# Attention inside a fused kernel: sums read out of PSUM at another place, softmax sums over groups of three tiles, and a new spread of small work over two engines

## The chip, the core and the metric

One core of one Trainium2 chip runs the whole program. The metric is device time in microseconds, the median of three runs of the compiled program. Where a profile is quoted, its times are microseconds from the first instruction of one profiled execution, and durations in groups are mean nanoseconds of one instruction. PE is TensorE's matmul side, PEld its weight loads, DVE is VectorE, ACT is ScalarE, POOL is GpSimd and SP issues transfers.

## The reference, cut to what matters

Attention comes first, then a mixture of experts, then a second feed-forward part. Only attention is touched. It has 2 x 8 heads, 1152 keys, 576 pooled queries and a head size of 64:

```python
q_pool = q.reshape(B, H, S // 2, 2, D).mean(axis=3)
scores = scale * np.matmul(q_pool, k.transpose(0, 1, 3, 2))
scores = scores - np.max(scores, axis=-1, keepdims=True)
attn = np.exp(scores)
attn = attn / (np.sum(attn, axis=-1, keepdims=True) + 1e-09)
return np.matmul(attn, v)
```

## The kernel before, in words

Heads are worked on in eight pairs, `p` 0 to 7. A pair has nine steps `t`, one for each tile of 128 keys; the loop over `g` at the end of the attention part runs through all of them and writes the program in the order in which the engines' queues will hold it. Each engine works its queue strictly in that order, so a waiting instruction holds up all that stands behind it.

In step `t` of pair `p` stand, in this order on PE: the scores of tile `t` (`scores`, eight products), two "chunks", the products of the previous tile's exponentials with `v` (`pv`, into the one PSUM buffer `pv` that a pair has), sometimes the sums of exponentials (`psums`), and the remaining chunks. ACT turns scores into exponentials `pt`.

A chunk (`max_chunk`) is a product of queries and keys of the *next* pair, from which the row maxima are found. There are 27 chunks to a pair, in units of three: nine units, four blocks of queries of head 0, four of head 1, and one of both heads' remainders (two products to a chunk). Of a unit's three chunks DVE reduces one (line 103), ACT takes the positive part of one (`wd<-mx`), and DVE joins the third with it (line 239, called `ISA` in the program's order and `CUSTOM_DVE_ANT_0` in the trace; a short read of the accumulator follows). The chunks lie in three PSUM buffers `mx`. When all are through, `max_cols` makes the maxima and their remainders on DVE (`mfin`, `Mt`), and in step 8 `max_rows` transposes them on PE (line 269) and copies them with ACT into `qb`, where the next pair's scores need them.

Work between the chunks is put there by a table: `at_step(p, t, ...)` gives step `t` of pair `p` a task, and each chunk slot takes one task ahead of its chunk; what is left over is done at the step's end. Tasks are the preparation of the next pairs' queries and keys (`qhi`, `qlo`, `khi`, `klo`, `kdiff`, `qcopy`), `max_cols`, the reciprocal of the sums and the output of the pair before (`sum_rec`, `x_out`), and the decoding of weights for a later stage (`decode`, three parts to a block, on DVE with one ACT instruction `dm<-wraw`). `qlo` writes the lower half of the query tile `qs` on DVE (line 97, `qs<-tq,qs`); a head's first chunk needs it. In the last pair there are no chunks, and three decode parts stand in each step.

The sums of exponentials need a product with a matrix of ones for each tile (`psums`, line 323: 16 PE records for one pass). To save passes, DVE adds tiles ahead (`st`): tiles 0 and 1, 2 and 3, 4 and 5. So a pair has six passes, three over `st` and three over tiles 6, 7 and 8. When the last tile is through, in step 0 of the next pair, `post_evac` moves products and sums out of `pv`: two ACT reads (`wd<-pv`, `sm<-pv`) and a DVE addition (`sm<-pv,sm`). The next pair's first `pv` product, in its step 1, has to wait for all three. Before the change this stands at the very end of step 0:

```python
for f in tasks:
    f()
if t == 0 and p > 0:
    post_evac(p - 1)
```

The functions and the loop:

Of the kernel before, what the change touches and what calls it, by code (L numbers as in the profile page):

```python
# [9 lines left out]
F32 = mybir.dt.float32  # L10
# [4 lines left out]
AF = mybir.ActivationFunctionType  # L15
ALU = mybir.AluOpType
# [68 lines left out]
def kernel(ctx, tc, cst, qt, kt, v, wgo, w1, w2, wio, out):  # L85
# [4 lines left out]
    def act(out, in_, func=AF.Copy, **kw):  # L90
        A.activation(out=out, in_=in_, func=func, **kw)  # L91

    def tt(eng, out, a, b, op):
        eng.tensor_tensor(out=out, in0=a, in1=b, op=op)  # L94
# [80 lines left out]
        SP.dma_start(out=vt[p], in_=v[p])  # L175

    DEC_M = 32
    DEC_T, DEC_A = [0, 1, 3, 5, 7, 8], 23
    tqt = {}

    def qsum(p, h):
# [13 lines left out]
    def qcopy(p, h):  # L195
        QB[p, h] = ap.tile([P, SQ], F32R, name="qb", bufs=NBL)
        act(QB[p, h][:64], QS[p, h][:64].bitcast(F32))

    def khi(p, h, c):
        if c == 0:  # L200
            At[p, h] = ap.tile([P, S], F32R, name="at", bufs=NB)
        cs_ = slice(c * SQ, (c + 1) * SQ)
        act(At[p, h][:, cs_], kd[p, h][:, cs_])

    def klo(p, h, c):
        cs_ = slice(c * SQ, (c + 1) * SQ)
        tt(G if 2 * p + h < 3 else V, Bt[(2 * p + h) % NBL][:64, cs_], kd[p, h][:64, cs_], At[p, h][:64, cs_].bitcast(F32), ALU.subtract)
# [33 lines left out]
    def ahead(units):  # L241
        n = len(units)
        seq_ = [(units[0], 0), (units[0], 1)]
        for i in range(n):
            if i + 1 < n:
                seq_ += [(units[i + 1], 1)]
            seq_ += [(units[i], 2)]
            if i + 1 < n:
                seq_ += [(units[i + 1], 0)]
        return [(*u, c) for u, c in seq_]  # L250

    chunks = ahead([(h, j) for h in range(2) for j in range(4)])
    mchunks = ahead([(0, 4)])
    chunks0 = ahead([(h, j) for h in range(2) for j in range(4)] + [(0, 4)])

    mfin = {}

# [47 lines left out]
            mm(pvt[p][64 * h:64 * h + 64, f, :HQ], lhsT=vt[p][:, t, h, :], rhs=Pt[p, t][:, h, f * HQ:(f + 1) * HQ], start=t == 0, stop=t == KT - 1, skip_group_check=True)  # L305


    twos = (1, 3, 5)
    St = {}

    def add_two(p, t):
        St[p] = ap.tile([P, 2, SQ], F32, name="st", bufs=1)
        tt(V, St[p], Pt[p, t - 1], Pt[p, t], ALU.add)

    def psums(p, t):


        for src in ([St[p]] if t - 1 in twos else []) + ([] if t in twos or t + 1 in twos else [Pt[p, t]]):
            for f in range(2):
                for h in range(2):  # L320
                    for a in range(2):
                        q_, t0 = 64 * h + 32 * a, 256 * a + 160 * f
                        mm(pvt[p][q_:q_ + 32, f, HQ:HQ + 160], lhsT=e2[:, h], rhs=src[:, h, t0:t0 + 160], start=False, stop=src is Pt.get((p, KT - 1)), skip_group_check=True)
# [108 lines left out]
    def load_raw(i, pool):  # L432
        f, c = divmod(i, 2)
        wraw[i] = pool.tile([P, 512, 2], I32, name="wraw", bufs=2)
        (SP if pool is ap else A).dma_start(out=wraw[i].rearrange("p a b -> p (a b)"), in_=wio[f, :, 512 * c:512 * (c + 1)].bitcast(I32))

    def decode(i, part, pool):
        f, c = divmod(i, 2)
        lo, hi = wraw[i][:, :, 0], wraw[i][:, :, 1]
        dst = wd[f][:, 512 * c:512 * (c + 1)]  # L440
        if part == 0:
            m = dmt[i] = pool.tile([P, 512], F32, name="dm", bufs=2)
            s = dst_[i] = pool.tile([P, 512], I32, name="ds", bufs=1)
            act(m, hi.bitcast(F32), AF.Abs)
            ts(V, s, hi, -0x80000000, ALU.bitwise_and)
        m, s = dmt[i], dst_[i]
        mi = m.bitcast(I32)
        if part == 1:
            ts(V, m, m, F_LO, ALU.max, F_HI, ALU.min)
            stt(s, lo, 29, s, ALU.logical_shift_right, ALU.bitwise_or)  # L450
        if part == 2:
            ts(V, mi, mi, 3, ALU.logical_shift_left, 0x40000000, ALU.bitwise_xor)
            stt(dst.bitcast(I32), mi, 0x7FFFFFFF, s, ALU.bitwise_and, ALU.bitwise_or)


    T_S, T_T, T_R, T_X = [2, 4, 5, 6]
    sched = {}

    def at_step(p, t, *fns):
        sched.setdefault(9 * p + t, []).extend(fns)  # L460
# [3 lines left out]
    at_step(-1, 4, lambda: (qcopy(0, 0), klo(0, 1, 1)))  # L464
    at_step(-1, 5, lambda: qcopy(0, 1))
    for p in range(NPAIR):
        for h, (a, b) in enumerate((((p - 2, 4), (p - 1, 0)), ((p - 1, 0), (p - 1, 3)))):
            lp, lt = (a[0], 2) if h == 0 else (p - 2, 6)
            if p == 0:
                continue  # L470
            if (p, h) == (1, 0):
                at_step(-1, 1, lambda: load_k(1, 0))
                at_step(-1, 6, lambda: (qsum(1, 0), khi(1, 0, 0), kdiff(1, 0)))
                at_step(-1, 7, lambda: qhi(1, 0))
                at_step(-1, 8, lambda: max_cols(0), lambda: qlo(1, 0))
                at_step(0, 0, lambda: khi(1, 0, 1), lambda: (klo(1, 0, 0), qcopy(1, 0)))
                at_step(0, 1, lambda: klo(1, 0, 1))
                continue
            at_step(lp, lt, lambda p=p, h=h: load_k(p, h))
            at_step(*((p - 2, 4 * h) if p > 1 else (lp, lt)), lambda p=p, h=h: load_q(p, h))  # L480
            at_step(a[0], a[1], lambda p=p, h=h: (qsum(p, h), khi(p, h, 0)))
            at_step(a[0], a[1] + 1, lambda p=p, h=h: (qhi(p, h), khi(p, h, 1), kdiff(p, h)))
            at_step(a[0], a[1] + 2, lambda p=p, h=h: qlo(p, h))
            at_step(b[0], b[1], lambda p=p, h=h: (klo(p, h, 0), qcopy(p, h)))
            at_step(b[0], b[1] + 1, lambda p=p, h=h: klo(p, h, 1))
        at_step(p - 1, 6, lambda p=p: load_v(p))
        if p:
            at_step(p - 1, 8, lambda p=p: max_cols(p))
        if p < NPAIR - 1:
            at_step(p + 1, T_R, lambda p=p: sum_rec(p))  # L490
            at_step(p + 1, T_X, lambda p=p: x_out(p, 0))
            at_step(p + 1, T_X + 1, lambda p=p: x_out(p, 1))
            at_step(p + 2, 1, lambda p=p: x_put(p))
# [68 lines left out]
    for g in range(-9, 9 * NPAIR):  # L562
        p, t = divmod(g, 9)
        if t == 0:
            todo = list(chunks if p >= 0 else chunks0) if p + 1 < NPAIR else []
            mtodo = list(mchunks) if 0 <= p < NPAIR - 1 else []
        tasks = list(sched.get(g, ()))
        if p >= 0 and t - 1 in twos:
            tasks += [lambda: None] * (2 - len(tasks))
            tasks.insert(2, lambda p=p, t=t: add_two(p, t - 1))  # L570
        if p == NPAIR - 1:
            tasks.append(lambda: [(raw_ahead(ap, DEC_A), decode_step(ap, DEC_A)) for _ in range(3)])
        elif p >= 0 and t in DEC_T:
            tasks.append(lambda: (raw_ahead(ap, DEC_A), decode_step(ap, DEC_A)))

        slot = [0]

        def mxc(todo=todo):
            if tasks:
                tasks.pop(0)()  # L580
            if todo:
                max_chunk(p + 1, *todo.pop(0))
            slot[0] += 1

        prev = divmod(g - 1, 9)
        seq = "0mmrpsmMt" if p < NPAIR - 1 else "0mmrpsmmt"
        if g < 0:
            seq = "mmmm"
        assert not (t == 8 and (todo or mtodo)), (p, len(todo), len(mtodo))
        if t < 3:  # L590
            seq = seq.replace("M", "m")
        for ch in seq:
            if ch == "0":
                if p >= 0:
                    scores(p, t)
            elif ch == "m":
                mxc()
            elif ch == "M":
                if mtodo:
                    mxc(mtodo)  # L600
                else:
                    mxc()
            elif ch == "s":
                if p > 0 and t == T_S:
                    sum_log(p - 1)
            elif ch == "t":
                if p > 0 and t == T_T:
                    sum_tr(p - 1)
            elif ch == "e":
                mxc([])  # L610
            elif ch == "r":
                if t == 8 and 0 <= p < NPAIR - 1:
                    max_rows(p + 1)
            elif ch in "pfg" and prev[0] >= 0:
                if ch in "pf":
                    pv(*prev, 0)
                if ch in "pg":
                    pv(*prev, 1)
                    psums(*prev)
        for f in tasks:  # L620
            f()
        if t == 0 and p > 0:
            post_evac(p - 1)
        if p > 0 and t in (T_X - 1, T_X):
            x_tr(p - 1, t - T_X + 1)
        if g == -1:
# [770 lines left out]
```

## Time and profile before

| | |
|---|---|
| median of 3 runs | 691.95 us (691.91 to 692.37) |
| the profiled execution | 689.39 us, its span 687.6 us |
| pairs 1 to 6, from one pair's transposes of maxima to the next | 205.06 us, 34.18 us each |
| busy in those: PE, DVE, ACT | 197.93, 154.73, 147.36 us |
| mean granted clock of the span | 0.988 of full speed, 1.00 in the pairs 1 to 6 |

Attention takes the first 298 us of the span. PE is the fullest engine in it, so it is read by PE's timeline: where PE stands still, and which instruction's end lets it go on. A start in the timeline less the start before it is what an instruction costs its engine; the duration in the row is longer where the next one overlaps. The times between pairs are the starts of line 269 in step 8: 20.96, 52.16, 86.20, 120.67, 154.66, 189.22, 223.49 and 257.22.

### The profile page before, as it was taken

To read this page: it belongs to the slowest core of one execution; us is meant where nothing else is said; L and a number is where in the kernel's file an instruction comes from. 1 tells how busy PE (TensorE), PEld (TensorE's weight loads), DVE (VectorE), ACT (ScalarE), POOL (GpSimd) and SP (SyncE) were. 2 spreads that over 40 slices of the span, in tenths; PEclk is the share of its full clock that TensorE was granted. 3 is DMA by queue.
4 is the path that set the end of the run, shared out by engine and by line. 5 is a ranking of instruction groups with operands and counts; after the bars stand their busy time and mean duration, and the time that the engine had idled before them with its cause. 6 is when DMAs were issued, how large, how long until landed. Compare 5 with 4: busy or idle time off the path is not lost. (4 is left out here: it accounts for less than half of the span.)

```text
span 687.6 us, 11646 instructions
## 1 busy us (share of the span) xinstructions
PE 636.9 (93%) x4335; PEld 499.2 (73%) x4335; DVE 498.4 (72%) x1035; ACT 401.6 (58%) x825; POOL 155.9 (23%) x155
## 2 busy tenths in 40 slices
PE   4899999999999999849989999987999999999997
PEld 3776767676767675528877977757787999999995
DVE  5686869686969686965753967514999977897775
ACT  7878585858585857514344546524665554555543
POOL 7500110101010000023222523302222332233222
PEclk9899999999999999989999999999999999999999
DMA  7853444444442313439489877660000020001001
GB/s 268 279 136 130 107 152 99 148 107 148 101 142 73 113 27 120 140 119 352 143 281 398 294 277 291 241 242 20 0 1 2 1 92 1 1 0 47 1 1 47
DMA packets 26643, 88.35 MB, mean 128 GB/s; under 512 B 2886, under 2 KB 7631, under 8 KB 22482
## 3 DMA queue, kind: packets, MB, share of 16 engines
q1 hardware_dynamic: 21264, 73.23, 30.4%
q0 software_dynamic: 3568, 8.79, 5.6%
q10 hardware_dynamic: 1746, 5.51, 2.4%
q8 instruction: 36, 0.59, 0.3%
q14 instruction: 29, 0.24, 0.1%
HBM read 79.65 MB, written 8.39 MB: 128 GB/s over the span
## 5 line engine op out<-in xcount | busy, mean ns | idle before, releaser
L91 ACT ACTIVATE pt<-sc 128x320 f32<-128x320 f32 (+1 forms) x216 | 96.1, 488 | 30.1 <-PE sc L290 25.8
L100 POOL TENSOR_SCALAR u<-u 128x384 f32<-128x384 f32 x48 | 60.3, 1257 | 151.9 <-ACT u L91 117.2
L305 PE MATMUL pv<-pt,vt 128*64 128x288 f32 x576 | 86.1, 420 | 7.3 <-issue 5.5
L866 PE MATMUL zps<-yh,wh 128*128 128x384 f32 x188 | 64.1, 341 | 1.7 <-DVE n L97 1.7
L868 PE MATMUL zps<-yl,wh 128*128 128x384 f32 x188 | 63.3, 337 | 0.0
L305 PEld LDWEIGHTS pv<-pt,vt 128*64 128x64 f32 x576 | 35.6, 136 | 37.9 <-issue 21.9
L867 PE MATMUL zps<-yh,wd 128*128 128x384 f32 x180 | 60.8, 338 | 0.0
L1306 PE MATMUL ops<-wh,gl 128*128 128x512 f32 x144 | 57.8, 403 | 2.9 <-DVE gl L94 2.4
L103 DVE TENSOR_REDUCE Mp<-mx 128x1 f32<-128x384 f32 x72 | 39.3, 552 | 24.6 <-PE mx L225 24.0
L1306 PE MATMUL ops<-wh,gh 128*128 128x512 f32 x144 | 56.8, 395 | 0.2 <-ACT gh L91 0.2
L239 DVE CUSTOM_DVE_ANT_0 wd<-mx,wd 128x384 f32<-128x384 f32 x63 | 34.8, 553 | 25.3 <-PE mx L225 16.7
L1306 PE MATMUL ops<-wd,gh 128*128 128x512 f32 x135 | 53.1, 394 | 0.0
L225 PE MATMUL mx<-at,qs 128*128 128x384 f32 x120 | 39.3, 374 | 9.1 <-DVE qs L97 7.7
L91 ACT ACTIVATE l<-n,two 128x384 f32<-128x384 f32 x48 | 29.5, 615 | 24.7 <-DVE n L97 24.7
L91 ACT ACTIVATE u<-zps 128x384 f32<-128x384 f32 x48 | 23.2, 483 | 33.3 <-PE zps L868 29.9
L97 DVE SCALAR_TENSOR_TENSOR l<-n,r 128x384 f32<-128x384 f32 x48 | 26.6, 554 | 19.1 <-ACT r L91 19.1
L91 ACT ACTIVATE wd<-mx 128x384 f32<-128x384 f32 x63 | 30.0, 488 | 15.4 <-PE mx L225 15.0
L100 DVE TENSOR_SCALAR dm<-dm 128x512 f32<-128x512 f32 x64 | 32.6, 510 | 7.7 <-ACT dm L91 7.6
L866 PEld LDWEIGHTS zps<-yh,wh 128*128 128x128 f32 x188 | 35.4, 188 | 3.7 <-ACT r L91 2.0
L333 POOL COPY xu<-wd 128x64 f32<-128x64 f32 x8 | 2.0, 255 | 157.9 <-ACT wd L91 157.9
L1306 PEld LDWEIGHTS ops<-wh,gl 128*128 128x128 f32 x144 | 27.0, 188 | 13.9 <-DVE gl L94 7.0
L91 ACT ACTIVATE gh<-n 128x384 fp32r<-128x384 f32 x48 | 24.8, 517 | 20.6 <-DVE n L97 20.2
(291 smaller groups left out, 1726.7 us busy)
## 6 DMA issues: line engine op xcount, KB each, us to landing
wt<-in_w SPq DMA_DIRECT2D x32, 1024.0 KB, 7.3
wraw<-in_wio SPq DMA_DIRECT2D x23, 512.0 KB, 4.2
kd<-in_kt SPq DMA_DIRECT2D x16, 576.0 KB, 3.7
vt<-in_v SPq DMA_DIRECT2D x8, 576.0 KB, 6.5
wraw<-in_wio ACTq DMA_DIRECT2D x9, 512.0 KB, 6.3
tq<-in_qt SPq DMA_DIRECT2D x12, 288.0 KB, 4.9
tq<-in_qt POOLq DMA_DIRECT2D x12, 288.0 KB, 4.5
pt<-in_qt SPq DMA_DIRECT2D x4, 576.0 KB, 5.7
```

The source lines that it names most:

```text
L91: A.activation(out=out, in_=in_, func=func, **kw)
L97: V.scalar_tensor_tensor(out=out, in0=a, scalar=s, in1=b, op0=op0, op1=op1)
L100: eng.tensor_scalar(out=out, in0=a, scalar1=s1, scalar2=s2, op0=op0, op1=op1)
L103: V.tensor_reduce(out=out, in_=in_, axis=AX.X, op=op)
L225: mm(ps, lhsT=QS[p, h][:, j * P:(j + 1) * P], rhs=keys(h), start=True, stop=True)
L239: V.tensor_tensor_reduce(out=r_, in0=ps, in1=r_, scale=1.0, scalar=-3.0e38, op0=ALU.add, op1=ALU.max, accum_out=Mp[p % 2][:, h, j, 1:2])
L305: mm(pvt[p][64 * h:64 * h + 64, f, :HQ], lhsT=vt[p][:, t, h, :], rhs=Pt[p, t][:, h, f * HQ:(f + 1) * HQ], start=t == 0, stop=t == KT - 1, ...
L333: G.tensor_copy(xu4[:, hp, 64 * b:64 * b + 64], xu[:, o:o + 64])
L866: mm(out_, lhsT=a, rhs=c, start=first, stop=False)
L867: mm(out_, lhsT=b_, rhs=c, start=False, stop=False)
L868: mm(out_, lhsT=a, rhs=d, start=False, stop=last_)
L1306: mm(opt[b_, j], lhsT=(g_, g_, gl_)[i], rhs=(wo, wl_, wo)[i], start=f == 0 and i == 0, stop=f == NF - 1 and i == 2)
```

## The change

`post_evac` goes from the end of step 0 to right behind the last `psums` pass in that step. The sums are formed in three groups of three tiles: DVE adds five times a pair (tiles 0 and 1, then 2 to them; 3 and 4, then 5; 6 and 7), and PE makes four passes (the three groups and tile 8 by itself). The 27 chunks go in groups of 3 and 4 over steps 0 to 7, where before they were done by step 6. Decode parts, query and key preparation, `qcopy`, the transposes of sums and the reciprocals change steps; `dm<-wraw` may stand ahead of its block.

```diff
-    DEC_T, DEC_A = [0, 1, 3, 5, 7, 8], 23
+    DEC_T, DEC_A = [0, 1, 2, 7, 7, 8], 23
+    ABS_T = [3, 6]
...
-    chunks = ahead([(h, j) for h in range(2) for j in range(4)])
-    mchunks = ahead([(0, 4)])
-    chunks0 = ahead([(h, j) for h in range(2) for j in range(4)] + [(0, 4)])
+    chunks = ahead([(h, j) for h in range(2) for j in range(4)] + [(0, 4)])
...
-    twos = (1, 3, 5)
+    adds = {2: True, 3: False, 5: True, 6: False, 8: True}
+    whole = {3: (0,), 6: (0,), 8: (0, 1)}
...
-    def add_two(p, t):
-        St[p] = ap.tile([P, 2, SQ], F32, name="st", bufs=1)
-        tt(V, St[p], Pt[p, t - 1], Pt[p, t], ALU.add)
+    def add_tile(p, t, new):
+        if new:
+            St[p] = ap.tile([P, 2, SQ], F32, name="st", bufs=1)
+        tt(V, St[p], Pt[p, t - 2] if new else St[p], Pt[p, t - 1], ALU.add)
...
-        for src in ([St[p]] if t - 1 in twos else []) + ([] if t in twos or t + 1 in twos else [Pt[p, t]]):
+        for src in [(St[p], Pt[p, t])[i] for i in whole.get(t, ())]:
...
-    T_S, T_T, T_R, T_X = [2, 4, 5, 6]
+    T_S, T_T, T_R, T_X = [2, 3, 4, 6]
...
-        for h, (a, b) in enumerate((((p - 2, 4), (p - 1, 0)), ((p - 1, 0), (p - 1, 3)))):
+        for h, (a, b) in enumerate((((p - 2, 6), (p - 1, 0)), ((p - 1, 1), (p - 1, 4)))):
...
-        seq = "0mmrpsmMt" if p < NPAIR - 1 else "0mmrpsmmt"
+        seq = "0mmrpsmt" if p < NPAIR - 1 and t in (0, 2, 4, 6, 7) else "0mmrpsmmt"
...
                     psums(*prev)
+                    if prev[1] == KT - 1:
+                        post_evac(prev[0])
         for f in tasks:
             f()
-        if t == 0 and p > 0:
-            post_evac(p - 1)
```

What this makes of the queues is seen in three places, all in pair 1.

ACT's queue in step 0, where `wd<-pv` and `sm<-pv` are `post_evac`'s reads and `pt` are exponentials. Before:

```order
L91 ACTIVATE qb<-qs 64x576
L91 ACTIVATE at<-kd 128x576
L91 ACTIVATE wd<-mx 128x384 x2
L91 ACTIVATE dm<-wraw 128x512
L91 ACTIVATE wd<-pv 128x576
L91 ACTIVATE sm<-pv 64x320
L91 ACTIVATE pt<-sc 128x320
```

And with the change:

```order
L91 ACTIVATE wd<-mx 128x384
L91 ACTIVATE wd<-pv 128x576
L91 ACTIVATE sm<-pv 64x320
L91 ACTIVATE dm<-wraw 128x512
L91 ACTIVATE wd<-mx 128x384
L91 ACTIVATE pt<-sc 128x320
```

Five instructions stood between the exponentials and the reads; now one does.

DVE's queue in the steps 2 and 3, around `qs<-tq,qs`, the lower half of head 1's queries for the next pair. Before:

```order
L103 TENSOR_REDUCE Mp_116<-mx 128x1
L97 SCALAR_TENSOR_TENSOR qs<-tq,qs 64x576
L239 ISA wd,Mp_116<-mx,wd 128x384
L239 ISA Mp_116 128x1
L94 TENSOR_TENSOR st<-pt 128x1152
L103 TENSOR_REDUCE Mp_116<-mx 128x1
```

And with the change, where the first `ISA` is that of the last chunk of step 2:

```order
L103 TENSOR_REDUCE Mp_116<-mx 128x1
L94 TENSOR_TENSOR st<-pt 128x1152
L240 ISA wd,Mp_116<-mx,wd 128x384
L240 ISA Mp_116 128x1
L100 TENSOR_SCALAR dm<-dm 128x512
L97 SCALAR_TENSOR_TENSOR wd<-dm,ds 128x512
L97 SCALAR_TENSOR_TENSOR qs<-tq,qs 64x576
L103 TENSOR_REDUCE Mp_116<-mx 128x1
L94 TENSOR_TENSOR st<-st,pt 128x1152
```

`qs` now stands behind an addition, a chunk and a decode part. On PE, head 1's first chunk (`kx,qs`) is the second chunk of step 3, and between it and the last chunk of step 2 stand eight score products and one chunk.

DVE's queue from the last chunk (the last `ISA` with `wd`) to the maxima `mfin` and `Mt`. Before:

```order
L94 TENSOR_TENSOR st<-pt 128x1152
L239 ISA wd,Mp_116<-mx,wd 128x384
L239 ISA Mp_116 128x1
L97 SCALAR_TENSOR_TENSOR qs<-tq,qs 64x576
L100 TENSOR_SCALAR dm<-dm 128x512
L97 SCALAR_TENSOR_TENSOR ds<-wraw,ds 128x512
L103 TENSOR_REDUCE mfin<-Mp_116 128x2x5
L100 TENSOR_SCALAR Mt_114<-mfin 128x5x2
L97 SCALAR_TENSOR_TENSOR Mt_114<-mfin,Mt_114 128x5x2
```

And with the change:

```order
L103 TENSOR_REDUCE Mp_116<-mx 128x1
L100 TENSOR_SCALAR ds<-wraw 128x512
L240 ISA wd,Mp_116<-mx,wd 128x384
L240 ISA Mp_116 128x1
L100 TENSOR_SCALAR dm<-dm 128x512
L97 SCALAR_TENSOR_TENSOR ds<-wraw,ds 128x512
L103 TENSOR_REDUCE mfin<-Mp_116 128x2x5
L100 TENSOR_SCALAR Mt_114<-mfin 128x5x2
L97 SCALAR_TENSOR_TENSOR Mt_114<-mfin,Mt_114 128x5x2
L97 SCALAR_TENSOR_TENSOR qs<-tq,qs 64x576
```

The rows look alike, but on PE this last chunk was in step 6 and is now the last of step 7, two products with the remainders, right ahead of step 8's eight score products and the transposes of `Mt`.

## Rows read from the trace of the kernel before

**Rows 1.** Busy time by engine, pairs 1 to 6, then pair 7 and the tail.

```profile
core 0: us, PE busy (x) PEld busy (x) DVE busy (x) ACT busy (x) POOL busy (x), PEclk, DMA share, GB/s
52.16:257.22 205.06, 197.93 (x1721) 137.65 (x1719) 154.73 (x361) 147.36 (x326) 20.12 (x26) 1.00 0.39 112
257.22:298.20 40.98, 33.08 (x319) 21.04 (x317) 31.73 (x78) 22.80 (x48) 0.65 (x2) 1.00 0.34 113
```

**Rows 2.** PE's timeline, pair 3, steps 0 to 3: start, duration, instruction, wait.

```profile
125.86 0.75 PE L323 MATMUL pv<-pt,e 128*32 128x160 f32 x16
126.54 0.44 PE L225 MATMUL mx<-kx,qs 128*128 128x384 f32 x1
...
129.69 1.19 PE L305 MATMUL pv<-pt,vt 128*64 128x288 f32 x8 [1.11 <-issue]
...
134.70 0.44 PE L225 MATMUL mx<-at,qs 128*128 128x384 f32 x1
134.98 0.33 PE L225 MATMUL mx<-kx,qs 128*128 128x384 f32 x1
135.15 0.31 PE L288 MATMUL sc<-qs,at 128*128 128x320 f32 x1
...
136.21 0.52 PE L225 MATMUL mx<-at,qs 128*128 128x384 f32 x2
```

**Rows 3.** ACT's timeline of the same place.

```profile
127.98 0.63 ACT L91 ACTIVATE wd<-pv 128x576 f32<-128x576 f32 x1
```

**Rows 4.** DVE's timeline of the same place.

```profile
129.10 0.48 DVE L94 TENSOR_TENSOR sm<-pv,sm 64x320 f32<-64x320 f32 x1 [1.24 <-ACT sm L91]
...
133.29 0.76 DVE L97 SCALAR_TENSOR_TENSOR qs<-tq,qs 64x576 fp32r<-64x576 f32 x1
```

**Rows 5.** PE's timeline, pair 3, steps 7 and 8.

```profile
152.26 0.75 PE L323 MATMUL pv<-st,e 128*32 128x160 f32 x16
...
153.48 0.42 PE L288 MATMUL sc<-qs,at 128*128 128x320 f32 x1
...
154.66 0.60 PE L269 MATMUL mx<-cs,Mt 128*34 128x128 f32 x4
```

**Rows 6.** PE's timeline, pair 0, step 0.

```profile
25.45 0.50 PE L225 MATMUL mx<-at,qs 128*128 128x384 f32 x1 [0.90 <-ACT at L91]
```

**Rows 7.** DVE's additions of exponentials in pairs 1 to 6, as a group.

```profile
L94 DVE TENSOR_TENSOR st<-pt 128x1152 f32<-128x1152 f32 x18 | 24.3, 1347 | 0.0
```

**Rows 8.** DVE's timeline, pair 2, a chunk and a decode part.

```profile
104.04 0.54 DVE L239 CUSTOM_DVE_ANT_0 wd<-mx,wd 128x384 f32<-128x384 f32 x1
...
104.52 0.41 DVE L100 TENSOR_SCALAR dm<-dm 128x512 int32<-128x512 int32 x1
...
105.58 1.01 DVE L103 TENSOR_REDUCE Mp<-mx 128x1 f32<-128x384 f32 x2
```

**Rows 9.** PE waits for qs at the start; DVE's row beside it.

```profile
12.07 1.08 DVE L97 SCALAR_TENSOR_TENSOR qs<-tq,qs 64x576 fp32r<-64x576 f32 x1 [0.17 <-ACT qs L91]
13.30 0.41 PE L225 MATMUL sc<-kx,qs 128*128 128x384 f32 x1 [1.72 <-DVE qs L97]
```

**Rows 10.** A chunk of two products on PE, and DVE's row that waits for it.

```profile
146.27 0.51 PE L229 MATMUL mx<-at,QM 128*128 128x384 f32 x2
146.93 0.56 DVE L239 CUSTOM_DVE_ANT_0 wd<-mx,wd 128x384 f32<-128x384 f32 x1 [1.43 <-PE mx L229]
```

**Rows 11.** DVE's timeline, pair 3, from a decode part to the maxima.

```profile
152.10 0.43 DVE L100 TENSOR_SCALAR dm<-dm 128x512 f32<-128x512 f32 x1
...
153.45 0.18 DVE L97 SCALAR_TENSOR_TENSOR Mt<-mfin,Mt 128x10 f32<-128x10 f32 x1
```

**Rows 12.** DVE's timeline at the end of attention: the last sums.

```profile
293.35 0.48 DVE L94 TENSOR_TENSOR sm<-pv,sm 64x320 f32<-64x320 f32 x1
```

**Rows 13.** A long DVE instruction, and POOL's instruction at that time.

```profile
101.83 2.29 DVE L94 TENSOR_TENSOR Bt<-kd,at 64x576 fp32r<-64x576 f32 x1
102.18 1.31 POOL L94 TENSOR_TENSOR kx<-kd 128x384 fp32r<-128x384 f32 x1
```

More of the change, by code (lines that the diff above doesn't have):

```diff
@@ L435, in load_raw, with decode_abs @@
         (SP if pool is ap else A).dma_start(out=wraw[i].rearrange("p a b -> p (a b)"), in_=wio[f, :, 512 * c:512 * (c + 1)].bitcast(I32))
+    def decode_abs(pool, i=None):
+        i = dec[0] + (dec[1] > 0) if i is None else i
+        if i not in dmt and i in wraw:
+            m = dmt[i] = pool.tile([P, 512], F32, name="dm", bufs=2)
+            act(m, wraw[i][:, :, 1].bitcast(F32), AF.Abs)
     def decode(i, part, pool):
@@ L441, in decode @@
         if part == 0:
-            m = dmt[i] = pool.tile([P, 512], F32, name="dm", bufs=2)
+            decode_abs(pool, i)
             s = dst_[i] = pool.tile([P, 512], I32, name="ds", bufs=1)
-            act(m, hi.bitcast(F32), AF.Abs)
             ts(V, s, hi, -0x80000000, ALU.bitwise_and)
@@ L475 @@
                 at_step(-1, 8, lambda: max_cols(0), lambda: qlo(1, 0))
-                at_step(0, 0, lambda: khi(1, 0, 1), lambda: (klo(1, 0, 0), qcopy(1, 0)))
+                at_step(0, 0, lambda: khi(1, 0, 1), lambda: klo(1, 0, 0))
                 at_step(0, 1, lambda: klo(1, 0, 1))
+                at_step(0, 4, lambda: qcopy(1, 0))
                 continue
@@ L483 @@
             at_step(a[0], a[1] + 2, lambda p=p, h=h: qlo(p, h))
-            at_step(b[0], b[1], lambda p=p, h=h: (klo(p, h, 0), qcopy(p, h)))
+            at_step(b[0], b[1], lambda p=p, h=h: klo(p, h, 0))
+            at_step(p - 1, 4 + h, lambda p=p, h=h: qcopy(p, h))
             at_step(b[0], b[1] + 1, lambda p=p, h=h: klo(p, h, 1))
@@ L564 @@
         if t == 0:
-            todo = list(chunks if p >= 0 else chunks0) if p + 1 < NPAIR else []
-            mtodo = list(mchunks) if 0 <= p < NPAIR - 1 else []
+            todo = list(chunks) if p + 1 < NPAIR else []
         tasks = list(sched.get(g, ()))
-        if p >= 0 and t - 1 in twos:
+        if p >= 0 and t in adds:
             tasks += [lambda: None] * (2 - len(tasks))
-            tasks.insert(2, lambda p=p, t=t: add_two(p, t - 1))
+            tasks.insert(2, lambda p=p, t=t: add_tile(p, t, adds[t]))
         if p == NPAIR - 1:
             tasks.append(lambda: [(raw_ahead(ap, DEC_A), decode_step(ap, DEC_A)) for _ in range(3)])
-        elif p >= 0 and t in DEC_T:
-            tasks.append(lambda: (raw_ahead(ap, DEC_A), decode_step(ap, DEC_A)))
+        else:
+            if p >= 0 and t in ABS_T:
+                tasks.append(lambda: (raw_ahead(ap, DEC_A), decode_abs(ap)))
+            if p >= 0:
+                tasks += [lambda: (raw_ahead(ap, DEC_A), decode_step(ap, DEC_A))] * DEC_T.count(t)
         slot = [0]
@@ L585 @@
         prev = divmod(g - 1, 9)
-        seq = "0mmrpsmMt" if p < NPAIR - 1 else "0mmrpsmmt"
+        seq = "0mmrpsmt" if p < NPAIR - 1 and t in (0, 2, 4, 6, 7) else "0mmrpsmmt"
         if g < 0:
             seq = "mmmm"
-        assert not (t == 8 and (todo or mtodo)), (p, len(todo), len(mtodo))
-        if t < 3:
-            seq = seq.replace("M", "m")
+        assert not (t == 8 and todo), (p, len(todo))
         for ch in seq:
@@ L597 @@
                 mxc()
[L598 to L602, printed above, removed]
             elif ch == "s":
```

## Prediction

> **What bounds the kernel now.** I read the busy time by stretch first. In the pairs 1 to 6 PE is busy for 197.93 of 205.06 us at full granted clock, DVE for 154.73, ACT for 147.36 [rows 1]. So PE sets the pace, one pair takes 205.06 / 6 = 34.18, and a pair gets shorter only if PE has less to do or stands still less. Next I read PE's timeline for places where it stands still. The large one repeats in each of these pairs: `pv`'s first product in step 1 waits 1.11 us [rows 2]. ACT's and DVE's rows show for what: the two reads and the addition of `post_evac` begin at 127.98 and 129.10, and `pv` starts at 129.69 [rows 3, 4]. Last come the margins that are not waits now but could become waits. `qs` ends at 133.29 + 0.76 = 134.05, and head 1's first chunk `kx` starts at 134.98, 0.9 later [rows 2, 4]. `Mt` ends at 153.45 + 0.18 = 153.63, and its transposes start at 154.66, 1.0 later [rows 5, 11]. These two margins are what the change spends.
>
> **The sums, fewer passes.** A pass that stands alone costs PE 126.54 - 125.86 = 0.68; the double one in step 7 costs 153.48 - 152.26 = 1.22 [rows 2, 5]. Before there are four alone and one double, 3.94 a pair; after it two alone and one double (the third group with tile 8), 2.58. PE has 1.36 less to do. For two passes the bounds are 1.08 (each as the second of a double, 0.54) and 1.5 (each as long as the row, 0.75); I take 1.36, the sum over the places where they stand. DVE pays for it with two more additions a pair, each 1.35 [rows 7]; DVE has 205.06 - 154.73 = 50.3 idle, 8.4 a pair [rows 1], which hides 2.7 where nothing waits for the queue. Where something does is the matter of the next but one part.
>
> **The read-out moved.** From the ACT row to the start of `pv` it takes 129.69 - 127.98 = 1.71 [rows 2 to 4], with about 0.1 ahead of it for the last sum to reach ACT, 1.8. Before, five other ACT instructions stood in front of it. Now PE meanwhile does a chunk (0.28), eight score products (136.21 - 135.15 = 1.06) and two chunks (about 0.4) [rows 2], together 1.7. Of the wait of 1.11 about 0.1 stays: 1.0 less. What is pushed back on ACT, the next exponentials, must free the score buffers for step 2; by the same rows they come about half a microsecond before they are needed, so I cost that at nothing, and at 0.3 a pair if the cover fails.
>
> **Head 1's first chunk.** `qlo` goes from step 2 to step 3 on DVE, and in the queue it now follows the last chunk of step 2 and a decode part. From that chunk's start on PE: a chunk of one product is ready for DVE 0.49 after it starts (0.66 for two products, 146.93 - 146.27, less the 0.17 of one) [rows 2, 10]. Its DVE instruction takes 0.48 and the decode part 1.06 (104.04 to 104.52 to 105.58) [rows 8], `qs` 0.76 [rows 4], and from its end to PE's start it was 13.30 - 12.07 - 1.08 = 0.15 [rows 9]. Sum 2.94. PE in that time has the chunk (134.98 - 134.70 = 0.28), eight scores (1.06) and one chunk (0.17) [rows 2], 1.51. So **a new wait of 1.43** in step 3, in front of which nothing can be done: `pv` and all that follows stand behind the chunk in PE's queue. The additions in step 2 stand ahead of the same chunk, but DVE reaches it some tenths before PE delivers it, so they don't lengthen the chain; without that slack of about 0.4 they would.
>
> **The maxima's transposes.** The last chunk, of two products, now stands at the end of step 7. DVE can begin 0.66 after it [rows 10], needs 0.48 for it [rows 8], and then has the decode part and the maxima, 153.45 - 152.10 + 0.18 = 1.53 [rows 11]: 2.67. PE has the two products (0.34) and eight scores (1.06), 1.40 [rows 2]. **A second new wait of 1.27**, in step 8. Behind it stand `pv` and the next pair's scores; their `qb` rows on ACT come later by as much and then just in time.
>
> **Weighing the shared port.** A `Bt` of DVE took 2.29 where 0.74 is usual, and it ended 0.63 after POOL's `kx` (102.18 + 1.31 = 103.49) [rows 13]; an instruction of DVE with two SBUF inputs stood still while POOL read. The added exponentials have two SBUF inputs too. By the row, such a block costs 1.55 on DVE once a pair, in the pairs 0 to 5 where `kx` still runs behind a transfer. The Trainium skill, "SBUF — State Buffer", section "Who interferes with whom", says that such an instruction and a GpSimd instruction that reads SBUF exclude each other, and that the one that issues first blocks the other fully. By that rule, with which the trace agrees in the 0.63 above, the two more additions of each pair are two more chances of a block, and the time would be the second rival's. In my order `kx` comes up while the second addition (step 3) runs, behind `qs`, so POOL is the one that waits; before, a block fell on the busy part of DVE and PE paid a part. I take off 0.8 in all, half of one block, for waits of PE that now swallow it (bounds 0 and, for four blocks, 6.2 either way).
>
> **Pair 0** has no `post_evac`, but its own wait of 0.90 for ACT in step 0 [rows 6]; with one chunk less there and `qcopy` gone from ACT's queue I let it vanish. 1.36 + 0.90 less, 2.70 more: +0.4. **Pair 7** has no chunks and so neither new wait. Its end is set by DVE, which works off decode parts and reaches the last `sm` at 293.35 [rows 12]; two more additions are 2.7 more there [rows 7]. DVE idles 40.98 - 31.73 = 9.3 in that stretch [rows 1], most of it at the two ends, and the earlier start of the pair gives back what the missing pass took. I take +0.4, nearer the end at which its idle time takes them in; bounds 0 and 2.7.
>
> **The sum.** A pair of 1 to 6: -1.36 - 1.0 + 1.43 + 1.27 = +0.34, six times +2.0. With pair 0 (+0.4), pair 7 (+0.4) and the port (-0.8): +2.0. All that follows attention is unchanged. The profiled execution's 689.39 would become 691.4; the median of the runs is 2.56 above it, and 691.95 + 2.0 = **694.0**.
>
> **The rivals.**
> *The transposes' wait is not paid*, the one on the other side. Its place is step 8, its price 1.27 in seven pairs, 8.9: 694.0 - 8.9 = 685.1. For it speaks that `mfin` has long been early (1.0) and that PE's chunks are now spread evenly; against it, that a decode part stands between the last chunk and `mfin` in the queue and DVE works strictly in order. It decides from a wait 0.5 shorter than I say: 7 x 0.5 is 3.5, and the kernel is faster by 0.2%.
> *DVE falls behind.* With 2.7 more a pair, a block of 1.55 by `kx` falls ahead of head 1's first chunk and lengthens that wait as it stands: in four of six pairs, 6.2, 700.2. For it speaks the long `Bt` [rows 13]; against it, that `kx` must first wait for its query transfer, which by the same start of the chain lands after `qs`.
> *Gains and waits cancel exactly*: 2.36 less and 2.36 more a pair, if both waits are about 0.17 shorter than computed, and the ends give nothing: 692.
>
> **How the numbers follow.** The forecast gets 0.50. Its own range is 691 to 697.5: each wait may be off by 0.25 in seven pairs. The first rival gets 0.22, the second 0.13, the third 0.15. A difference of 0.2%, 1.4 us, is about what a measurement can tell. The forecast ends slower by more in 0.33, within it in 0.16 and faster in 0.01; the first rival is faster in 0.20 and within in 0.02; the second is slower in 0.13; the third is within in 0.13 and beyond it by 0.01 on each side. Faster 0.22, same 0.31, slower 0.47. The range goes down to 688, which leaves out about half of the first rival and more (0.12 in all), and up to 698.5, which leaves out half of the second (0.07).
>
> **What would show it.** `pv`'s wait in step 1 at 0.1 to 0.2. A wait of PE for DVE's `qs` of about 1.4 ahead of a `kx` chunk in step 3, and one for `Mt` of about 1.3 at line 269 in step 8, in the pairs 0 to 6. PE records of sums down from 768 to 512 and `st` up from 24 to 40. Pairs at 34.2 to 34.6. If pairs are at 33 or less, one of the two waits is missing and I have read the order wrongly; if they are above 35, DVE was late for other reasons.

## The result and the profile after

The changed kernel takes 696.15 us (median of five runs, 695.37 to 698.19) against 691.95; the ratio is 1.0065, interval 1.0045 to 1.0086. It is slower by 0.65%, where 0.3% (694.0) was forecast. The profiled execution of after took 698.19, the highest of its five, and the one of before 689.39, the lowest shown. So the two traces differ by 8.8 in span, the medians by 4.2.

Busy time by stretch of after, in the columns of [rows 1]: pairs 1 to 6, then pair 7 and the tail.

```profile
53.03:262.79 209.76, 194.75 (x1526) 133.58 (x1526) 168.01 (x373) 146.17 (x328) 20.17 (x26) 0.98 0.39 109
262.79:305.88 43.09, 34.68 (x286) 21.95 (x287) 36.63 (x84) 22.00 (x48) 0.65 (x2) 0.91 0.34 111
```

PE has 3.2 us less to do than in [rows 1], DVE 13.3 more, and the pairs take 4.7 more; pair 7 and the tail take 2.1 more. The same view pair by pair (pairs 1, 2, 3, 5 and 6) tells two kinds of pairs apart:

```profile
53.03:89.42 36.39, 33.63 (x255) 22.84 (x255) 27.09 (x61) 25.19 (x57) 3.96 (x5) 0.95 0.42 115
89.42:123.92 34.50, 31.89 (x254) 21.90 (x254) 28.33 (x63) 24.55 (x55) 3.96 (x5) 1.00 0.45 125
123.92:158.42 34.50, 31.89 (x254) 21.91 (x254) 28.16 (x63) 24.55 (x55) 3.97 (x5) 1.00 0.45 125
192.92:229.07 36.15, 33.54 (x255) 23.06 (x255) 27.83 (x63) 24.54 (x55) 3.11 (x4) 0.95 0.35 103
229.07:262.79 33.72, 31.93 (x255) 21.95 (x255) 28.25 (x65) 22.79 (x51) 1.20 (x2) 1.00 0.21 63
```

Three pairs (2 to 4; two are shown) take 34.50 each, 0.32 above the mean of before, 34.18, where the forecast had +0.34. Two take 36.39 and 36.15 at a mean clock of 0.95; their PE is busy 1.7 longer with nearly the same instructions. Pair 6 takes 33.72, as it did before (33.73). The pairs of before were not alike either; here are its pairs 2 and 3:

```profile
86.20:120.67 34.47, 33.08 (x288) 22.91 (x286) 26.04 (x62) 24.86 (x55) 3.95 (x5) 1.00 0.44 125
120.67:154.66 33.99, 32.81 (x289) 22.90 (x287) 25.12 (x62) 24.85 (x55) 3.96 (x5) 1.00 0.45 127
```

PE's timeline of pair 3 shows the waits (in [rows 2] `pv` waits 1.11, and nothing waits in step 3 or, [rows 5], at the transposes):

```profile
128.44 0.75 PE L324 MATMUL pv<-st,e 128*32 128x160 f32 x16
...
131.54 1.19 PE L304 MATMUL pv<-pt,vt 128*64 128x288 f32 x8
...
139.64 0.41 PE L226 MATMUL mx<-kx,qs 128*128 128x384 f32 x1 [1.46 <-DVE qs L97]
...
158.42 0.40 PE L268 MATMUL mx<-cs,Mt 128*34 128x128 f32 x2 [1.14 <-DVE Mt L97]
```

`pv`'s wait in step 1 is gone. (In before it was 1.10 or 1.11 in the pairs 1 to 5, but 0.73 in pair 6, so the prediction's "in each of these pairs" holds for five of six.) In its place stand 1.46 or 1.47 for `qs` in the pairs 1 to 6 (1.86 in pair 0) and 1.14 for `Mt` in five of seven pairs (0.32 in the other two). DVE's timeline says what is late in each:

```profile
137.07 0.56 DVE L240 CUSTOM_DVE_ANT_0 wd<-mx,wd 128x384 f32<-128x384 f32 x1 [0.26 <-ACT wd L91]
...
137.56 0.42 DVE L100 TENSOR_SCALAR dm<-dm 128x512 int32<-128x512 int32 x1
138.01 0.69 DVE L97 SCALAR_TENSOR_TENSOR wd<-dm,ds 128x512 int32<-128x512 int32 x1
138.73 0.76 DVE L97 SCALAR_TENSOR_TENSOR qs<-tq,qs 64x576 fp32r<-64x576 f32 x1
...
156.37 0.56 DVE L240 CUSTOM_DVE_ANT_0 wd<-mx,wd 128x384 f32<-128x384 f32 x1 [1.33 <-PE mx L230]
...
156.85 0.42 DVE L100 TENSOR_SCALAR dm<-dm 128x512 f32<-128x512 f32 x1
157.19 0.68 DVE L97 SCALAR_TENSOR_TENSOR ds<-wraw,ds 128x512 int32<-128x512 int32 x1
157.79 0.17 DVE L103 TENSOR_REDUCE mfin<-Mp 128x10 f32<-128x20 f32 x1
```

Twice the same picture: the last chunk, a decode part (1.17 and 0.94), then what PE waits for.

The long pairs 1 and 5 have their clock fall right behind the `qs` wait (69.04 and 208.64); so has pair 0. Windows of after:

```profile
65.00:69.00 4.00, 2.57 (x18) 1.54 (x14) 3.30 (x7) 2.90 (x8) 0.00 (x0) 1.00 0.88 254
69.00:73.00 4.00, 3.96 (x16) 2.50 (x17) 2.73 (x5) 1.23 (x3) 1.80 (x2) 0.58 0.37 115
73.00:77.00 4.00, 4.00 (x39) 2.85 (x39) 2.47 (x12) 2.29 (x5) 0.11 (x1) 0.99 0.41 65
209.00:213.00 4.00, 4.00 (x19) 2.84 (x19) 2.99 (x9) 1.10 (x3) 1.91 (x2) 0.58 0.45 144
```

In pair 7, which has no chunks, PE waits 3.35 for an addition, where at the same place in before it waited 1.56. DVE's timeline marks no idle time from 283.67 to the last `sm`'s wait. PE's row in before, then PE's row and DVE's timeline in after:

```profile
284.90 0.75 PE L323 MATMUL pv<-st,e 128*32 128x160 f32 x16 [1.56 <-DVE st L94]
```

```profile
291.07 0.91 PE L324 MATMUL pv<-st,e 128*32 128x160 f32 x16 [3.35 <-DVE st L94]
```

```profile
285.34 1.35 DVE L94 TENSOR_TENSOR st<-pt 128x1152 f32<-128x1152 f32 x1
...
288.34 0.69 DVE L97 SCALAR_TENSOR_TENSOR wd<-dm,ds 128x512 int32<-128x512 int32 x1
289.06 0.69 DVE L94 TENSOR_TENSOR wd<-mx,rc 128x512 f32<-128x512 f32 x1
289.67 1.35 DVE L94 TENSOR_TENSOR st<-st,pt 128x1152 f32<-128x1152 f32 x1
...
300.80 0.48 DVE L94 TENSOR_TENSOR sm<-pv,sm 64x320 f32<-64x320 f32 x1 [1.31 <-ACT sm L91]
```

The last `sm` comes 38.0 after the pair's start (262.79), before 36.1 after it [rows 12, 1]. Behind the 3.35 the granted clock stands at 0.50 from about 291.5 to 298.4; in before it did not fall at this place:

```profile
291.00:299.00 8.00, 7.93 (x64) 4.83 (x68) 7.90 (x18) 2.73 (x5) 0.00 (x0) 0.57 0.34 111
```

DVE is late first, but at the end it is DVE's last `sm` that waits 1.31 for PE's last products, by way of ACT.

### The profile page after: what moved, and what is told of

Same layout as the page of the kernel before. It is cut to its first block, busy times and chain, and to the rows that moved or that the text cites. A ratio compares the mean times of both kernels' runs of the same rounds, so it can differ in the third digit from the quotient of the medians.

```text
span 696.4 us, 11178 instructions
## 1 busy us (share of the span) xinstructions
PE 638.5 (92%) x4079; PEld 497.1 (71%) x4079; DVE 516.8 (74%) x1051; ACT 399.1 (57%) x825; POOL 154.9 (22%) x155
## 5 line engine op out<-in xcount | busy, mean ns | idle before, releaser
L304 PE MATMUL pv<-pt,vt 128*64 128x288 f32 x576 | 88.9, 432 | 0.6 <-DVE sm L94 0.5
L226 PE MATMUL mx<-at,qs 128*128 128x384 f32 x120 | 43.3, 389 | 7.1 <-ACT at L91 6.9
L91 ACT ACTIVATE u<-zps 128x384 f32<-128x384 f32 x48 | 23.2, 483 | 33.1 <-PE zps L871 30.2
L226 PEld LDWEIGHTS mx<-at,qs 128*128 128x128 f32 x120 | 23.2, 203 | 20.3 <-issue 7.3
L871 PEld LDWEIGHTS zps<-yl,wh 128*128 128x128 f32 x188 | 35.4, 189 | 0.0
```

Of the source, the lines that this page charges most:

```text
L226: mm(ps, lhsT=QS[p, h][:, j * P:(j + 1) * P], rhs=keys(h), start=True, stop=True)
L871: mm(out_, lhsT=a, rhs=d, start=False, stop=last_)
```

## The experiments

Each was timed against the kernel before on the same chip; these ratios stand beside the change's 1.0065. Beside them before ran 81 times, in three groups, and took 687.5 to 698.8 (medians 693.1 to 694.3). "Pairs" is the mean of the pairs 1 to 6, from the starts of the transposes: before 34.18, after 34.96.

**One new wait out: x1_qlo_back.** Head 1's `qlo` goes back to step 2.

```diff
-            at_step(a[0], a[1] + 2, lambda p=p, h=h: qlo(p, h))
+            at_step(a[0], a[1] + 2 - h, lambda p=p, h=h: qlo(p, h))
```

> The changed kernel with head 1's lower query half written in step 2 again. Theory A (the two new waits of PE, and the clock that falls behind them, are the loss): PE's wait of 1.46 for it in step 3 goes in seven pairs, 10 less, and with it the falls of the granted clock in two pairs, 2 x 1.8: about 683 against 696. Theory B (the two more additions load DVE, and PE waits for DVE wherever it stands): the wait turns up at the next product that needs DVE, and the time stays within 3 of 696.

Ratio 0.9939 (0.9913 to 0.9965), pairs 33.84. The `qs` wait is gone, and no window of the pairs 0 to 6 is below full clock; the `Mt` wait stays at 1.14 in four pairs (1.48 in pair 5, 0.32 or 0.33 in the others). The median, 689.4, lies between the two theories: the pairs 2 to 4 take 33.9 instead of 34.5, so of the wait of 1.46 only 0.6 was gained.

**The other out: x2_decode_late.** One decode part goes behind the maxima.

```diff
-    DEC_T, DEC_A = [0, 1, 2, 7, 7, 8], 23
+    DEC_T, DEC_A = [0, 1, 2, 7, 8, 8], 23
```

> The changed kernel with the decode part that stands between the last chunk and the maxima put into step 8, behind them. Theory A: the wait of 1.14 for Mt in step 8 falls by the part's 0.94, in five to seven pairs, 5 to 6.6 less: about 690. Theory B: DVE is later by as much in the next pair's step 0, and PE waits there: within 2 of 696.

Ratio 0.9974 (0.9946 to 1.0003), pairs 34.28. The `Mt` wait falls to 0.33, the `qs` wait stays at 1.46, and the clock falls behind it in three pairs; the pairs at full clock take 33.7, shorter by the whole 0.81, near theory A's 0.94. PE's row of x2 at the transposes of pair 3:

```profile
158.15 0.29 PE L268 MATMUL mx<-cs,Mt 128*34 128x128 f32 x1 [0.33 <-DVE Mt L97]
```

**Both out: x3_both.** Both edits.

> Both edits together. Theory A: what is left is the gain alone, 1.36 and 1.0 a pair less than the kernel before: pairs of about 32, 15 to 18 less than before in all, 675 to 679. Theory B: DVE needs 28.3 of a pair of 34.5 already, and at 32 its queue is late for several chunks: not under 688.

Ratio 0.9857 (0.9823 to 0.9892), pairs 33.18. The two edits add up (34.96 less 1.12 less 0.68 is 33.16), and together they make the kernel faster than before. But the median, 684.5, lies between the two theories, and the gain is smaller than the waits: 34.50 to 33.10 in pair 3 is 1.40, and the waits shrank by 1.46 + 0.81 = 2.27. PE's timeline of x3_both, pair 3, steps 3 and 4:

```profile
133.91 0.55 PE L351 MATMUL mx<-cs,sm 128*128 128x128 f32 x3 [0.21 <-DVE Mp L103]
...
135.21 0.31 PE L296 MATMUL sc<-qb,Bt 66*128 66x320 f32 x1
135.65 0.44 PE L226 MATMUL mx<-kx,qs 128*128 128x384 f32 x1
136.11 0.44 PE L226 MATMUL mx<-at,qs 128*128 128x384 f32 x1
136.49 0.71 PE L304 MATMUL pv<-pt,vt 128*64 128x288 f32 x4
```

From the start at 135.21 to that at 136.49 it takes 1.28, where the same four starts took 0.59 in after: 0.69 is lost in gaps that the view does not mark, and 0.41 more between the `pv` ahead of them and 135.21. I read this so: while PE stood for `qs`, DVE caught up with the chunks; without the standstill PE meets DVE's backlog one step later.

**Old sums in the last pair alone: x6_last_pairwise.** Pair 7 takes its groups of two back.

```diff
+    adds_last = {2: True, 4: True, 6: True}
+    whole_last = {2: (0,), 4: (0,), 6: (0, 1), 7: (1,), 8: (1,)}
...
+        adds_p = adds_last if p == NPAIR - 1 else adds
```

> The changed kernel with sums of two tiles as before in the last pair alone, three additions and six passes there. If DVE's queue in the last pair is what makes PE wait 3.35 for st and drops the clock to half for 7 us behind it, the wait falls to about 1.5, the clock stays, and the whole is 2 to 4 shorter, about 693. If the end is set by the decode parts and the transfers alone, it stays within 1 of 696.

Ratio 1.0029 (0.9995 to 1.0063). The 3.35 becomes two waits of 0.85 and 0.81, and pair 7 with the tail takes 41.04 instead of 43.09, all at full clock:

```profile
259.57:300.61 41.04, 33.00 (x317) 21.14 (x318) 34.48 (x82) 22.13 (x48) 0.97 (x2) 1.00 0.37 117
```

By the trace the groups of three cost the 2.05 there, by the longer wait and the fall of the clock behind it together; the ratio alone is not sure of it.

**The parts alone in the old spread: x4, x5, x8.** The kernel before with the read-out moved, with the groups of three, and with both.

```diff
                     psums(*prev)
+                    if prev[1] == KT - 1:
+                        post_evac(prev[0])
```

> The kernel before, with one part of the change alone: the read-out of products and sums stands right behind the last sums. Theory A (this part is worth what the prediction says, and the two new waits ate it up in the change): the wait of pv in step 1 is gone, the wait of PE for DVE's qs and the one for Mt do not appear, since the old spread is kept; pairs 1 to 6 about 1.0 us shorter (33.1 to 33.3), seven such places, ratio to before about 0.990 (0.988 to 0.993). Theory B (the read-out gives nothing, because ACT's exponentials behind it come later and the scores' buffers with them): pairs as before, 34.2, a new wait of PE for ACT in step 2 or 3, ratio 0.997 to 1.003.

> The kernel before, with groups of three tiles alone, in the old spread of work. Theory A (DVE's queue is full from step 1 to step 5 in the old spread, though it has idle time elsewhere): PE has 1.1 us less to do in a pair, as the change's rows showed, but the addition in step 3 stands in a stretch where DVE has no idle time, so PE waits for DVE there for part of it; pairs 33.4 to 34.0, ratio to before 0.991 to 0.998. Theory B (idle time of DVE anywhere in the pair hides it): no new wait, pairs at 33.0 to 33.2, ratio about 0.988. The last pair loses 1 to 2 us to the additions by both.

> The kernel before, with the read-out behind the last sums and groups of three tiles, and the old spread of chunks, decode parts and preparation. Theory A (the new spread, not the two gains, brought the two new waits): no wait of PE for qs of 1.4 us in step 3 and none of 1.1 for Mt; pairs at 32.4 to 33.2, with some wait of PE for DVE in steps 2 to 5, ratio to before 0.980 to 0.988, near the version with both waits taken out (0.9857). Theory B (the new spread is needed to carry the additions): PE waits for DVE by 1 us or more a pair at another place, pairs at 33.8 or more, ratio above 0.990.

x4: 1.0019 (0.9987 to 1.005), pairs 34.54; x5: 0.998 (0.9952 to 1.0008), 34.41; x8: 1.0019 (0.9989 to 1.0048), 34.38. Theory A fell in x4 and x8; x5's ratio lies at its edge, its pairs above it: hardly any gain shows in the old spread. PE's timeline of x4, pair 3, the same steps as [rows 2]:

```profile
129.22 1.19 PE L305 MATMUL pv<-pt,vt 128*64 128x288 f32 x8
131.13 0.91 PE L225 MATMUL mx<-at,qs 128*128 128x384 f32 x2 [0.71 <-DVE Mp L239]
...
135.53 0.44 PE L225 MATMUL mx<-at,qs 128*128 128x384 f32 x1 [0.28 <-DVE Mp L239]
```

The 1.11 ahead of `pv` became 0.71 and 0.28 ahead of the next chunks, for whose buffers DVE is late. The timelines show what has changed: first a decode part of DVE in before, then the same part in x4 with what stands ahead of it, then a row of POOL in x4:

```profile
125.15 0.42 DVE L100 TENSOR_SCALAR ds<-wraw 128x512 int32<-128x512 int32 x1
```

```profile
128.31 0.48 DVE L94 TENSOR_TENSOR sm<-pv,sm 64x320 f32<-64x320 f32 x1 [2.65 <-ACT sm L91]
128.82 1.77 DVE L100 TENSOR_SCALAR ds<-wraw 128x512 int32<-128x512 int32 x1
```

```profile
129.01 1.30 POOL L94 TENSOR_TENSOR kx<-kd 128x384 fp32r<-128x384 f32 x1
```

The read-out's addition now stands ahead of the decode part and holds DVE's queue for 2.65; the part behind it then meets POOL's `kx` and takes 1.77 instead of 0.42. In the pairs 1 to 5 of x4 and x8 it takes 1.74 to 1.78 and ends 0.28 to 0.30 after `kx`. In pair 6 of x4 `kx` is nearly over when the part begins, and it takes 0.54; there PE waits 0.71 for ACT's `wd` in place of the 0.73 for `pv`, and the pair takes 34.00 instead of 33.73. So ACT, theory B's cause, shows in one pair, though not by the exponentials. In x5 `kx` holds up a `Bt` (2.11 to 2.36 instead of 0.74) in the pairs 1, 2, 4 and 5, and PE waits 0.39 to 0.95 for DVE's `Mp` behind it; the 0.58 for ACT's `wd` stands in all six. Pair 3, without such a `Bt`, takes 33.74 against 33.99. So in the old spread the gains don't arrive; what they would be there without the meetings with `kx`, no run shows.

**The parts undone in the new spread: x7, y1, y2.** x7 is x3_both with x6's last pair; y1 is x7 with the read-out at the end of step 0, y2 is x7 with sums of two in every pair.

```diff
-                    if prev[1] == KT - 1:
-                        post_evac(prev[0])
...
+        if t == 0 and p > 0:
+            post_evac(p - 1)
```

> The kernel after, with head 1's qlo a step earlier, one decode part moved behind the maxima, and the old sums of two tiles in the last pair alone. Theory A (the three losses of the change are apart from one another and add up): pairs as in the version with both waits out (33.1), and the last pair's end about 2 us shorter than there; ratio to before 0.983, 0.979 to 0.987, the fastest of all. Theory B (the last pair's end is set by DVE's decode parts, whatever the additions): no shorter than with both waits out, ratio 0.986.

> The version with both waits out and the old sums in the last pair (ratio 0.9855, pairs 33.20), with the read-out put back to the end of step 0. Theory A (in the new spread the place of the read-out is worth what DVE's queue lets through): two reads move behind two ACT instructions, wd at 0.35 and dm at 0.6, so pv waits 0.6 to 1.0 us in step 1; some of it is given back in step 4, where DVE no longer holds PE up as long; pairs 33.5 to 34.0, ratio 0.988 to 0.995. Theory B (the place of the read-out is worth nothing in this spread either, as in the old one): pairs 33.2, ratio 0.985.

> The same version with sums of two tiles in all pairs, not only in the last. Theory A (the fewer passes are worth less than PE's 1.36 us, since the additions hold DVE up in the steps 2 to 4): DVE has 2.7 us less to do and PE 1.36 more; the waits of PE for DVE in step 4, 1.0 in all, go; pairs 33.4 to 33.8, ratio 0.987 to 0.992. Theory B (the additions are hidden in DVE's idle time): pairs longer by the whole 1.36, 34.5, ratio 0.997.

x7: 0.9855 (0.9814 to 0.9896), pairs 33.20, and the end 41.39 from the last transposes, 43.07 in x3_both; the ratio cannot tell its two theories apart, the trace bears out A. y1: 0.9897 (0.9867 to 0.9927), 33.54, with a wait of 0.67 for `sm` back in step 1, as in pair 3:

```profile
126.46 0.46 PE L304 MATMUL pv<-pt,vt 128*64 128x288 f32 x2 [0.67 <-DVE sm L94]
```

y2: 0.9929 (0.9895 to 0.9963), 33.95. Here the read-out is worth 0.34 a pair and the groups 0.75, against 1.0 and 1.36 on PE; y2 lies a little above what I expected and well below theory B.

**The wait doubled: y3_qs_wait_doubled.** The kernel after, with more decode ahead of `qs`.

```diff
-    DEC_T, DEC_A = [0, 1, 2, 7, 7, 8], 23
+    DEC_T, DEC_A = [0, 1, 2, 2, 2, 8], 23
```

> The kernel after, with both decode parts of step 7 put ahead of qs, 0.35 and 1.06 us of DVE. The qs wait of PE in step 3 becomes 2.9 us, the Mt wait in step 8 falls to 0.3: by the waits alone a pair is 34.50 + 1.41 - 0.81 = 35.1, less what the longer standstill gives back in step 4. Theory A (the granted clock falls behind the standstill, the more surely the longer it is): falls to half for about 4 us behind it in most of the pairs, pairs near 37, ratio 1.015 to 1.03. Theory B (the falls have nothing to do with this wait): falls in at most two pairs, pairs 35.1, ratio 1.005 to 1.012.

Ratio 1.032 (1.0269 to 1.0371), pairs 37.78. The wait is 2.86 (3.24 in pair 0), `Mt`'s is 0.33. Windows of y3, pairs 2 to 4:

```profile
93.94:131.70 37.76, 34.57 (x254) 23.70 (x254) 27.62 (x63) 24.59 (x56) 3.97 (x5) 0.91 0.41 114
131.70:169.38 37.68, 34.48 (x255) 23.62 (x255) 27.62 (x63) 24.60 (x56) 3.96 (x5) 0.91 0.42 114
169.38:207.00 37.62, 34.43 (x254) 23.57 (x254) 27.61 (x63) 24.58 (x56) 3.96 (x5) 0.91 0.41 115
```

The clock falls in all seven pairs, for 6 to 7 us instead of the 4 expected, so the time lies a little above theory A. PE's busy time for the same 254 instructions is 34.5 instead of 31.89: the fall costs 2.6 a pair on top of the wait.

**DVE relieved in step 2: y4_decode_out_of_step_2.** x7 with the decode part of step 2 in step 6.

```diff
-    DEC_T, DEC_A = [0, 1, 2, 7, 8, 8], 23
+    DEC_T, DEC_A = [0, 1, 6, 7, 8, 8], 23
```

> The version with both waits out and the old sums in the last pair, with the decode part of step 2 moved to step 6, where DVE idles 0.9 us. Theory A (the 1.0 us of small waits in step 4 is DVE's queue, full from step 1 on): those waits go and pairs fall from 33.20 to 32.3 to 32.7, ratio 0.976 to 0.982. Theory B (they come from the buffers of the chunks or from ACT): pairs as before, 33.2, ratio 0.985.

Ratio 0.9836 (0.9788 to 0.9883), pairs 32.97: not told apart from x7 by time, and short of theory A. Pair 6 alone reaches 32.00; the pairs 2 to 5 take 33.1 to 33.4. DVE's, POOL's and PE's timelines of y4, pair 3, show what stands there:

```profile
131.58 2.42 DVE L94 TENSOR_TENSOR st<-st,pt 128x1152 f32<-128x1152 f32 x1
```

```profile
131.45 1.32 POOL L94 TENSOR_TENSOR kx<-kd 128x384 fp32r<-128x384 f32 x1
```

```profile
134.53 0.44 PE L226 MATMUL mx<-kx,qs 128*128 128x384 f32 x1 [0.56 <-DVE Mp L240]
```

The addition takes 2.42 instead of 1.35, begins while POOL's `kx` runs, and ends 1.23 after it (134.00 against 132.77), as if it did nearly all of its work behind it; in the pairs 1 to 5 it takes 1.96 to 2.68 and ends 1.22 or 1.23 after `kx`. Pair 6, which has no `kx` there, has an addition of 1.35 and no such wait.

## Why the prediction was right, and where its sizes were off

**Head 1's first chunk** and **the maxima's transposes**: right by place, cause and nearly by size, 1.46 for 1.43 and 1.14 for 1.27 (the latter in five pairs, not seven). That 1.46 came so close has some luck in it: by the starts DVE's chain took 3.16 where 2.94 was reckoned, and PE's own work 1.70 where 1.51 was. Of the 1.14 the decode part accounts for 0.81 (x2). Taking the two out makes the kernel faster than before, so they decide the sign.

**The read-out moved**: the wait on PE went from 1.11 to nothing, where 0.1 was to stay; the cover of the exponentials held, since PE's timeline marks no wait for ACT in its place.

**The sums, fewer passes**: PE's rows give exactly the 2.58 computed (one double of 1.22, two of 0.68); records went from 768 to 512, `st` from 24 to 40. With the other terms at their measured sizes, -1.36 - 1.11 + 1.46 + 1.14 is +0.13; pair 3 takes 34.50 against 33.99, +0.51. The rest is not in waits but in the chunks: by the starts, all chunks of this pair cost PE 6.75 before and 7.27 after, in 16 groups instead of 14, and another product (`mx<-wd,wbd`) gives 0.14 back. The forecast had the chunks' cost unchanged.

What was wrong in both gains is their meaning: I took them as time that a pair loses or wins by itself. The runs give them 0.34 and 0.75 once the waits are out, and nothing in the old spread, where PE's next waits, for the chunks' buffers, stand right behind. DVE, which empties most of these buffers, has little room there. In before, pair 3, steps 3 to 5, its busy time (the third in each row) is 3.97 and 3.91 of 4 us:

```profile
137.00:141.00 4.00, 4.00 (x41) 2.85 (x39) 3.97 (x9) 2.47 (x6) 1.01 (x1) 1.00 0.73 187
141.00:145.00 4.00, 4.00 (x32) 2.85 (x28) 3.91 (x16) 3.22 (x8) 0.00 (x0) 1.00 0.64 223
```

How much of the lost gain in x4, x5 and x8 is this full queue and how much the instructions held up beside `kx`, no run separates. The sentence that 8.4 idle a pair hides the additions "where nothing waits for the queue" was followed up only ahead of head 1's first chunk, and PE waits for the chunks' buffers too.

**Weighing the shared port**: the 0.8 taken off is near what the rows show. In before a `Bt` is held up in the pairs 2 and 4 (2.29 and 2.39), PE waits 0.21 and 0.30 for DVE's `Mp` behind it, and these pairs take 34.47 and 34.56 where pair 3, without it, takes 33.99: 1.05 in both together. In after no `Bt` of these pairs is held up; `ls` was (1.39, 1.20 and 1.41 in the pairs 2 to 4, against 0.29 in pair 6), and PE did not wait for it. By the rule of the Trainium skill, "SBUF — State Buffer", "Who interferes with whom", an addition can be blocked by `kx` in the same way; in y4, where the order brings the two together, the 2.42 agrees. That the one that issues first blocks the other does not come out of the starts in [rows 13]: `Bt` begins 0.35 ahead of `kx` and is the one held up. It was a matter of order, as the rival *DVE falls behind* had it; its place was not reached in the changed kernel, but in x4, x5 and x8 such meetings are there.

**Pair 0**: +0.53 for +0.4, by luck: its waits were 1.86 and 0.32 where 1.43 and 1.27 were reckoned, and the clock fell in it in both traces (25 to 29 in before, 35 to 39 in after). **Pair 7**: +2.1 for +0.4, inside the bounds of 0 and 2.7, and the value taken was at the wrong end. I set DVE's 9.3 idle against the additions without looking where PE's next pass stands: behind an addition that queues after three decode parts and more. And it is not DVE's queue alone that sets the end, as I had it, but also PE at half clock behind the wait.

**Not in the sum**: the clock. In the profiled execution the pairs 1 and 5 lose some 3.4 by it (PE's busy time of 33.63 and 33.54 against 31.89). Between the two traces this is the largest part of what the +2.0 lacked, with pair 7. In all, the span's 8.8 are 0.3 at the start, 0.5 in pair 0, 4.7 in the pairs 1 to 6 (some 3.4 of it the clock), 2.1 in pair 7 and 1.1 behind attention, where nothing was changed. What the last part is stays open, and how many falls the other four executions had is not recorded; their mean clocks are 0.970 to 0.981, that of the profiled one is 0.972. The trace of before is a calm one: its mean clock is 0.988, and in the 81 other executions of before it is 0.972 to 0.993, 0.980 in the mean. So how much of the 4.2 between the medians is the clock is not shown. That 696.15 lies well inside 691 to 697.5 owes something to luck, since neither the clock nor most of pair 7's loss was in the sum.

## What to carry to other kernels

A wait that is removed is worth only the distance to the next one: before summing gains, look for what the waiting engine meets in the next few steps, here the queue of the engine that empties its buffers. An instruction put earlier also puts later what stands behind it in another engine's queue: look for what that now runs beside, as the decode part and `kx` in x4. When a piece of work is put ahead of an operand, follow the chain from the last thing that operand's engine must finish, as both new waits could be computed to within 0.15 that way. And a wait on TensorE may cost more than its length, as those of 1.46 did here in 4 of 18 places, so a new one deserves a margin on the slow side.

## What the runs showed of the hardware

The granted clock fell from full speed to 0.50, that is 1.2 GHz, right behind some of PE's waits. Behind the `qs` waits of after, x2 and x6 it fell in three, three and one of seven pairs: each time in pair 0 (1.86 to 2.05), and in 4 of the 18 places with 1.46 to 1.48. In y3 (2.86 and 3.24) it fell in all seven. It stayed there for some 3 to 4 us in the former, some 6 to 7 in y3. No window of the pairs 0 to 6 showed it in x1, x3, y1 and y4, without the `qs` wait. The five waits of 1.10 or 1.11 for `pv` in before and the fourteen of 1.14 for `Mt` in after, x1 and x6 never brought one, nor did the 1.48 for `Mt` in x1, though one of 0.90 in pair 0 of before did [rows 6], which the same wait in x4, x5 and x8 did not. In pair 7 the clock fell in or within 1.5 us behind the wait for `st` in each kernel where it was long (2.85 in y3, 3.15 to 3.49 in after, x1, x2, x3, x5 and x8), and did not there in x6, x7, y1, y2 and y4, with waits of 0.85 at most. Why some waits of 1.46 bring a fall and others of the same length don't, these runs do not tell.

Many DVE instructions that met POOL's `kx` took longer than their like elsewhere: the decode part `ds<-wraw` 1.77 instead of 0.42 (x4), the addition 2.42 instead of 1.35 (y4), `Bt` 2.29 instead of 0.74 [rows 13], and each of these ended behind `kx`. Not all did: in pair 3 of before a `Bt` begins 0.39 ahead of `kx` and takes its usual 0.74. No run moved such a meeting by itself, so this is a reading of the traces.
